# Row-wise attention norms from the fourth token block on, in a fused linear-attention and two-layer MLP kernel on one Trainium2 core

## The chip, the core and the metric

The kernel runs on one core of a Trainium2 chip. A core has a matrix engine (TensorE, PE in the profile, with PEld for its weight loads), a vector engine (VectorE, DVE), a scalar engine (ScalarE, ACT), GpSimd (POOL) and SyncE (SP). Here POOL and SP do almost nothing but issue DMAs. Every engine works through its own instructions in program order and waits on semaphores for the others. The metric is the time on the device in microseconds; lower is better.

## The reference

```python
def _attn_ref(q, k, v, g_norm):                       # q, k, v: (8 batches, 8 heads, 576, 64) fp32
    kv = np.einsum('bhsd,bhse->bhde', k, v)           # 64x64 for each batch and head
    out = np.einsum('bhsd,bhde->bhse', q, kv)
    rms = np.sqrt(np.mean(out * out, axis=-1, keepdims=True) + 1e-06)
    return out / rms * g_norm                         # norm over the 64 values of a head

# x = attention output as (4608 tokens, 512); w_in (512, 2048), w_out (2048, 512), alpha (2048)
def _moe_ref(x, w_in, w_out, alpha):
    h = x @ w_in
    g = np.maximum(h, 0.0) + alpha * np.minimum(h, 0.0)
    return g @ w_out
```

## The kernel before

All matrix work is in fp16 with fp32 sums. The 4608 tokens are cut into nine blocks of 512 (`w` = 0 to 8; a batch has 576 tokens, so blocks and batches do not line up). The main loop `for w in range(1, NW)` runs 16 units `u` in each block. A unit does, in this program order:

- `m1_group(w, g)` (L391, L398, L402): four 128x512 matmuls give one 128-wide slice of the hidden layer in a PSUM bank. ACT takes the negative part (`m_sb`), DVE adds `beta * m_sb` to the bank and writes `gt`. From block 2 on two banks alternate, so the matmuls of unit u+2 wait until DVE has written `gt` of unit u.
- `unit_sums` and seven `prod_mm` (L546): the second layer of block w-1, written as seven half-size products over sums of tiles of `gt` and of `w_out`. `s_sum` makes the sums on DVE. Results collect in banks X, Y and Z, and `y_read` takes them out: `p1` and `c11` on ACT, `u2`, `u3`, `c22`, `c21` and `c12` on DVE. `Y_READS` says at which units; outputs are stored by SP.
- `attention(w + 1, u)`: one step of the attention of the next block. For each of the four head pairs: `step_kv` (five 128x128 matmuls and a masked multiply on DVE, L335), `step_ot` (the attention output with features on partitions, 128x512, L349, and its square on ACT, L355), and `step_ssq` (a 128x512 matmul with the block mask `mask16` sums the squares over each head and spreads the sums over its 64 partitions, L365; ACT turns them into `rstd`, L367; DVE multiplies output, `g_norm` and `rstd` into `xt`, L375).

The steps lie at units 3j+1, 3j+3 and 3j+5 for pair j. Batch w+2 is loaded by `load_gated` on POOL's queue: the remainder rows of q, then k, q and v. From batch 3 on q is turned by five DMA transposes on SP's queue (`dma_t`, L317), issued together at unit 11 of block w. POOL's next `load_gated` begins with the remainder rows of q, whose buffer the last of those five transposes must have read. ACT regroups k by pairs (`REG_AT`).

Block 0 is written out by hand. At the end of its first layer, after the hidden slice 14, DVE regroups k of batch 1 and clears a part of a k buffer, then writes `gt` of slice 15, whose bank a run of block 0's second layer needs.

The order on every engine is the order of the program text (`manual_schedule`); no planner moves anything.

Of the kernel before, what the change touches and what calls it, by code (L numbers as in the profile page):

```python
# [9 lines left out]
FP32 = mybir.dt.float32  # L10
FP16 = mybir.dt.float16
AF = mybir.ActivationFunctionType
ALU = mybir.AluOpType
# [4 lines left out]
def kernel(  # L18
# [11 lines left out]
    nc = tc.nc  # L30
# [5 lines left out]
    P = 128  # L36
# [11 lines left out]
    NC = D_MODEL // P  # L48
    assert NC == NPAIR and 0 < REM < P and P0 <= P and H % 4 == 0
    B_NAT = 3  # L50
    inv_d = 1.0 / D

    const_p = ctx.enter_context(tc.tile_pool(name="constp", bufs=1))
# [67 lines left out]
    bufs = []  # L121
    for i in range(NBUF):
        t = {}
        for nm in ("k", "v", "q"):
            n = 1 if nm == "v" else T0 if i == 0 else NT
            t[nm] = qkv_p.tile([P, n, H, D], FP16, name=f"{nm}sb{i}")
            if i > 0 or nm == "v":
                nc.vector.memset(t[nm][REM:P, n - 1, :, :], 0.0)
        bufs.append(t)
# [26 lines left out]
            )  # L156

    def buf_of(b, nm):
        return bufs[1 if nm == "q" and b >= B_NAT else b % NBUF][nm]

    def load_rem(b, nm):
        nc.gpsimd.dma_start(  # L162
# [2 lines left out]
        )  # L165

    def regroup(b, nm, h0, h1, eng=None):
        dst = bufs[b % NBUF][nm][:, 0:TPP, h0:h1, :].rearrange("p t h d -> p h t d")
        src = stages[b, nm][:, h0:h1, :, :]
        if eng is nc.scalar:  # L170
            nc.scalar.copy(out=dst, in_=src)
        else:
            (eng or nc.vector).tensor_copy(out=dst, in_=src)

    def load_batch(b, names=("k", "v", "q")):
        for nm in names:
            load_rem(b, nm)
            load_main(b, nm)
# [30 lines left out]
    def load_w_in(i):  # L209
# [4 lines left out]
        )  # L214
        w_in_sb.append(t)

    def load_w_out(i):
        t = w_p.tile([P, GW, D_MODEL], FP16, name=f"w_out_sb{i}")
        nc.gpsimd.dma_start(
            out=t[:],  # L220
            in_=moe_w_out[i * GW * P : (i + 1) * GW * P, :].rearrange("(g p) m -> p g m", p=P),
        )
        w_out_sb.append(t)
# [25 lines left out]
    load_batch(1, ("v",))  # L249
    load_w_out(2)  # L250
    load_w_out(3)
    load_batch(2, ("q", "k", "v"))


    warm_ps = ps_q.tile([P, W], FP32, name="warm_ps", tag="q")
# [18 lines left out]
    def pair_cols(b, nm, j):  # L274
        def f(t):
            n = rows(b)
            if nm == "v" and b == 0:
                h = 2 * j % HH
                return stages[b, nm, 2 * j // HH][0:n, h : h + 2, t, :]
            if nm == "v" and t < TPP:  # L280
                return stages[b, nm][:, 2 * j : 2 * j + 2, t, :]
            if nm == "v":
                return bufs[b % NBUF][nm][0:n, 0, 2 * j : 2 * j + 2, :]
            return bufs[b % NBUF][nm][0:n, t, 2 * j : 2 * j + 2, :]
        return f

    def step_t(b, j, pool=(ps_s, "s")):
        qs = pair_cols(b, "q", j)
        qt_ps = pool[0].tile([P, n_runs(b) * rows(b)], FP16, name="qt_ps", tag=pool[1])
        c = 0  # L290
        for t in range(n_runs(b)):
            n = rows(b)
            nc.tensor.matmul(  # L293
                out=qt_ps[:, c : c + n],
                lhsT=qs(t),
                rhs=ident16[0:n, 0:n],
                is_transpose=True,
                start=(t == 0),
                stop=(t == n_runs(b) - 1),
            )  # L300
            c += n
        if j == 0:
            qt_all[b] = attn_p.tile([P, NPAIR, S], FP16, name="qt_all")
        qts[b, j] = qt_all[b][:, j, :]
        if b == 0 and j < 2:
            nc.vector.tensor_copy(out=qts[b, j], in_=qt_ps[:, 0:S])
        else:
            nc.scalar.copy(out=qts[b, j], in_=qt_ps[:, 0:S])

    qt_all = {}  # L310

    def dma_t(b):
        qt = attn_p.tile([P, NPAIR, S], FP16, name="qt_all")
        for t in range(NT):
            c0, c1 = t * P, min((t + 1) * P, S)
            src = stages[b, "q"][:, t] if t < TPP else buf_of(b, "q")[0:REM, TPP]
            nc.sync.dma_start_transpose(  # L317
                out=qt[:, :, c0:c1], in_=src.rearrange("p h d -> p (h d)"),
            )
        for j in range(NPAIR):  # L320
            qts[b, j] = qt[:, j, :]

    def step_kv(b, j, pool=(ps_s, "s")):
        ks, vs = pair_cols(b, "k", j), pair_cols(b, "v", j)
# [37 lines left out]
    def ssq_mm(w, j, pool=(ps_s, "s")):  # L362
        ot_ps, sq = ots.pop((w, j))
        ssq_ps = pool[0].tile([P, W], FP32, name="ssq_ps", tag=pool[1])
        nc.tensor.matmul(out=ssq_ps[:], lhsT=mask16[:], rhs=sq[:], start=True, stop=True)  # L365
        rstd = attn_p.tile([P, W], FP32, name="rstd")
        nc.scalar.activation(  # L367
            out=rstd[:], in_=ssq_ps[:], func=AF.Abs_reciprocal_sqrt, bias=eps_t[:], scale=inv_d,
        )
        ots[w, j] = (ot_ps, rstd)  # L370

    def norm(w, j):
        ot_ps, rstd = ots.pop((w, j))
        xts[w, j] = xt_p.tile([P, W], FP16, name="xt", tag=f"xt{j}")
        nc.vector.scalar_tensor_tensor(  # L375
            out=xts[w, j][:], in0=ot_ps[:], scalar=g2col[:], in1=rstd[:],
            op0=ALU.mult, op1=ALU.mult,
        )

    gts = {}  # L380
# [8 lines left out]
    def m1_mm(h_ps, w, g, cs):  # L389
        for c in cs:  # L390
            nc.tensor.matmul(  # L391
                out=h_ps[:], lhsT=w_in_blk(c, g), rhs=xts[w, c][:],
                start=(c == 0), stop=(c == NC - 1),
            )

# [193 lines left out]
    Y_LIST = [(n, i) for n in Y_ORDER for i in range(2 * NK)]  # L589
    PER = len(Y_LIST) // NF  # L590
    Y_READS = {2: ("p1",), 5: ("u2",), 7: ("c11",), 9: ("u3",), 11: ("c22",), 14: ("c21",)}
    G_ORDER = [0, 1, 8, 9, 2, 3, 10, 11, 4, 5, 12, 13, 6, 7, 14, 15]


# [64 lines left out]
    ssq_mm(0, 3, h_at(2))  # L659
    norm(0, 2)  # L660
    norm(0, 3)
    first = [ps_h.tile([P, W], FP32, name="h_ps", tag=f"h{g}") for g in range(3)]
    for c in range(3):
        for g in range(2):
# [6 lines left out]
    for g in range(3, NF):  # L671
        m1_group(0, g, {3: S_POOL, 4: O_POOL, 5: O_POOL, 6: Q_POOL}.get(g))
        if g == 14:
            regroup(1, "k", 0, H)
            nc.vector.memset(bufs[0]["k"][REM:P, TPP, :, :], 0.0)


    ys = {}
# [66 lines left out]
    }  # L745

    def unit_sums(w, u):
        for back, n, k in S_AT.get(u, ()):
            if 1 <= w + back < NW:
                s_sum(w + back, n, k)  # L750

# [9 lines left out]
            ATT_1.setdefault(at, []).append((what, j))  # L761
    ATT = {"t": step_t, "kv": step_kv, "ot": step_ot, "ssq": step_ssq}

    def attention(w, u):
        if w < NW:
            for what, j in (ATT_1 if w == 2 else ATT_AT).get(u, ()):
                if what == "t" and w >= B_NAT:
                    continue
                if w < B or what in ("ot", "ssq"):
                    if w == 2 and what in ("kv", "ssq"):  # L770
                        pool = Q_POOL if j % 2 == 0 else S_POOL
                        (step_kv if what == "kv" else step_ssq)(w, j, pool)
                    else:
                        ATT[what](w, j)

    REG_AT = {8 + 2 * j: (("k", j),) for j in range(NPAIR)}

    Y3_AT = [(8, 8), (8, 8), (8, 8), (8, 9), (9, 9), (9, 10), (10, 10), (10, 10), (10, 11), (11, 11), (11, 12), (12, 12), (12, 13), (13, 14), (14, 16), (16, 16)]
    REG_2 = {2 * j: (("k", j),) for j in range(NPAIR)}
# [1 line left out]
    for w in range(1, NW):  # L781
        if w + 2 < B:
            load_gated(w + 2)
        for u in range(NF):
            m1_group(w, G_ORDER[u])
            if w > 1:
                unit_sums(w, u)
            if w == 1 and u == 2:
                regroup(2, "k", 0, H)
            if w == 1 and u == 3:  # L790
                dma_t(3)
            if w == 2 and u == 0:
                h_tags[0] = ("h1", "h2")
                h_turn[0] = 1
            if w > 2 and u == 0:
                y_read(w - 2, "c12")
            if w == 1:
                for i in range(*Y3_AT[u]):
                    y_mm(ys[3], 0, 3, i)
                    if i == NF - 1:  # L800
                        y_out(ys[3], 0, 3)
            else:
                for i in range(u * PER, (u + 1) * PER):
                    prod_mm(w - 1, *Y_LIST[i])
                for what in Y_READS.get(u, ()):
                    y_read(w - 1, what)
            attention(w + 1, u)
            if w == 1:
                for k in {5: (0,), 7: (1,)}.get(u, ()):
                    s_sum(1, 1, k)  # L810
                    s_sum(1, 2, k)
            if w + 2 < B:
                for nm, j in REG_AT.get(u, ()) if w > 1 else ():
                    regroup_pair(w + 2, nm, j)
                if u == 11 and w > 1:
                    dma_t(w + 2)
            if w == 2:
                for nm, j in REG_2.get(u, ()):
                    regroup_pair(3, nm, j)
                if u < 2:  # L820
                    s_sum(1, u + 1, 2)
# [48 lines left out]
```

## Time and profile before

| what | value |
|---|---|
| median of 3 runs | 282.61 us (282.56 to 283.07) |
| profiled execution | 282.48 us, span 280.7 us |
| PE busy | 274.0 us (98%), 1888 matmuls |
| DVE busy | 219.9 us (78%) |
| ACT busy | 157.0 us (56%) |
| granted TensorE clock | 1.0 |

The time of an execution is 1.8 us above the span of its profile. Blocks 2 to 6 take 28.9 us each in the trace, block 7 27.8 us. Busy times are merged, and an instruction's duration is longer than its distance to the next one on the same engine, since instructions overlap in the pipeline: a 128x512 matmul is shown with 379 ns and follows its neighbour after 216 ns. Sums over time are therefore made with distances between starts, not with durations.

### The profile page before, as it was taken

How to read it: one execution, taken by the hardware profiler on the slowest of the kernel's cores; microseconds unless marked ns; L12 is line 12 of the kernel's file. 1: busy time of each engine (PE TensorE's matmuls, PEld its weight loads, DVE VectorE, ACT ScalarE, POOL GpSimd, SP SyncE). 2: the span in 40 equal slices, each digit the busy share in tenths (PEclk: the TensorE clock that was granted, in tenths of full speed). 3: DMA queues.
4: the chain of work that ended last, by engine and by line, in shares of the span. 5: the costliest groups of instructions: out<-in, count | busy, mean ns of one | idle time of the engine just before them, and what ended most of it. 6: DMA issues, size and time to landing. Idle time of an engine off the chain costs nothing.

```text
span 280.7 us, 4978 instructions
## 1 busy us (share of the span) xinstructions
PE 274.0 (98%) x1888; PEld 173.8 (62%) x1888; DVE 219.9 (78%) x418; ACT 157.0 (56%) x268; POOL 61.9 (22%) x85
## 2 busy tenths in 40 slices
PE   7899999999999999999999999999999999999995
PEld 3444444555666676666666666666666666666784
DVE  6668729898788877887889787978887888787872
ACT  3567437788676545764576456745564566443310
POOL 8843332740720046007300450000000000000000
PEclk9999999999999999999999999999999999999999
DMA  8999999999793469947953697330112011201223
GB/s 163 199 207 196 197 201 193 191 140 169 91 171 69 104 72 165 152 112 120 165 91 97 121 152 122 93 106 1 40 37 75 2 37 37 77 0 37 77 76 114
DMA packets 77628, 31.37 MB, mean 112 GB/s; under 512 B 45780, under 2 KB 77284, under 8 KB 77604
## 3 DMA queue, kind: packets, MB, share of 16 engines
q0 software_dynamic: 55600, 18.85, 58.8%
q1 hardware_dynamic: 21108, 11.25, 15.0%
q10 hardware_dynamic: 896, 0.95, 1.0%
q8 instruction: 15, 0.25, 0.4%
q14 instruction: 9, 0.07, 0.1%
HBM read 36.71 MB, written 9.44 MB: 164 GB/s over the span
## 4 chain that ended last, share of the span: by engine, by line
PE 92%; DMA 5%; DVE 1%; ACT 0%; issue 0%; DVEq 0%
PE h_ps L391 42%; PE yY L546 15%; PE yZ L546 10%; PE yX L546 10%; DMA vst<-in_v_dram 5%; PE kv_ps L327 3%; PE ot_ps L349 3%; PE ssq_ps L365 3%; PE y L416 2%; PE warm_ps L259 2%; PE qt_ps L293 1%; DVE xt L375 1%; ACT rstd L367 0%; DVE kv_sb L335 0%; DVE ksb L193 0%
## 5 line engine op out<-in xcount | busy, mean ns | idle before, releaser
L391 PE MATMUL h_ps<-xt,w_in_sb 128*128 128x512 f16 x576 | 145.2, 379 | 0.2
L402 DVE SCALAR_TENSOR_TENSOR gt<-m_sb,beta_sb,h_ps 128x512 f16<-128x512 f32 x144 | 106.9, 746 | 39.9 <-ACT m_sb L398 38.1
L398 ACT ACTIVATE m_sb<-h_ps 128x512 f32<-128x512 f32 x144 | 86.0, 598 | 74.8 <-PE h_ps L391 60.2
L391 PEld LDWEIGHTS <-w_in_sb 128*128 128x128 f16 x576 | 54.8, 98 | 46.4 <-issue 1.0
L546 PEld LDWEIGHTS <-s 128*128 128x128 f16 x512 | 50.1, 98 | 19.3
L546 PEld LDWEIGHTS <-gt 128*128 128x128 f16 x384 | 37.6, 98 | 14.8
L546 PE MATMUL yY<-wsum,s 128*128 128x256 f16 x256 | 36.3, 273 | 0.0
L546 PE MATMUL yX<-w_out_sb,gt 128*128 128x256 f16 x256 | 35.1, 273 | 0.0
L355 ACT ACTIVATE sq_sb<-ot_ps 128x512 f16<-128x512 f32 x36 | 21.2, 598 | 16.7 <-PE ot_ps L349 16.6
L367 ACT ACTIVATE rstd<-ssq_ps,eps_t 128x512 f32<-128x512 f32 x36 | 24.7, 690 | 9.7 <-PE ssq_ps L365 9.2
L375 DVE SCALAR_TENSOR_TENSOR xt<-ot_ps,g2col,rstd 128x512 f16<-128x512 f32 x36 | 26.6, 745 | 3.2 <-ACT rstd L367 3.2
L162 POOL DMA_DIRECT2D qsb<-in_q_dram x7 | 4.9, 699 | 78.3 <-DMA qt_all<-qsb 76.3
L153 POOL DMA_DIRECT2D qst<-in_q_dram x20 | 17.7, 922 | 1.9 <-DMA vst<-in_v_dram 1.9
L546 PE MATMUL yZ<-wsum,s 128*128 128x256 f16 x128 | 17.6, 273 | 0.0
L546 PE MATMUL yZ<-w_out_sb,s 128*128 128x256 f16 x128 | 17.6, 273 | 0.0
L546 PE MATMUL yY<-wsum,gt 128*128 128x256 f16 x128 | 17.6, 273 | 0.0
L416 PE MATMUL y<-w_out_sb,gt 128*128 128x512 f16 x64 | 16.8, 379 | 0.5 <-DMA w_out_sb<-in_moe_w_out_dram 0.5
L349 PE MATMUL ot_ps<-qt_all,kv_sb 128*128 128x512 f16 (+7 forms) x64 | 13.6, 286 | 0.4 <-DVE kv_sb L335 0.3
L498 DVE TENSOR_TENSOR s<-s,gt 128x512 f16<-128x512 f16 x32 | 13.5, 421 | 0.5
L327 PEld LDWEIGHTS <-ksb 128*128 128x128 f16 (+1 forms) x164 | 11.5, 98 | 3.7 <-DVE ksb L193 1.1
L365 PE MATMUL ssq_ps<-sq_sb,mask 128*128 128x512 f16 x36 | 13.6, 379 | 0.1
L496 DVE TENSOR_TENSOR s<-gt 128x512 f16<-128x512 f16 x32 | 13.3, 419 | 0.1
(66 smaller groups left out, 206.6 us busy)
## 6 DMA issues: line engine op xcount, KB each, us to landing
out_dram<-y_sb SPq DMA_DIRECT2D x19, 256.0 KB, 2.2
kst<-in_k_dram POOLq DMA_DIRECT2D x7, 512.0 KB, 7.8
vst<-in_v_dram POOLq DMA_DIRECT2D x7, 512.0 KB, 9.9
qst<-in_q_dram POOLq DMA_DIRECT2D x20, 128.0 KB, 7.2
w_out_sb<-in_moe_w_out_dram POOLq DMA_DIRECT2D x4, 512.0 KB, 16.1
out_dram<-y_sb SPq DMA_DIRECT2D x25, 64.0 KB, 4.2
w_in_sb<-in_moe_w_in_dram POOLq DMA_DIRECT2D x3, 512.0 KB, 11.6
out_dram<-y_sb SPq DMA_DIRECT2D x9, 128.0 KB, 2.1
```

What stands on the lines that cost most here:

```text
L153: nc.gpsimd.dma_start(out=st[:, t, :, :], in_=srcs["q"][b, :, t * P : (t + 1) * P, :].rearrange("h p d -> p h d"),)
L327: nc.tensor.matmul(out=kv_ps[:], lhsT=ks(t), rhs=vs(t), start=(t == 0), stop=(t == n_runs(b) - 1),)
L349: nc.tensor.matmul(out=ot_ps[:, n0 - w * W : n1 - w * W], lhsT=kvs[b, j][:], rhs=qts[b, j][:, n0 - b * S : n1 - b * S], start=True, stop=True,
L355: nc.scalar.activation(out=sq[:], in_=ot_ps[:], func=AF.Square)
L365: nc.tensor.matmul(out=ssq_ps[:], lhsT=mask16[:], rhs=sq[:], start=True, stop=True)
L367: nc.scalar.activation(out=rstd[:], in_=ssq_ps[:], func=AF.Abs_reciprocal_sqrt, bias=eps_t[:], scale=inv_d,)
L375: nc.vector.scalar_tensor_tensor(out=xts[w, j][:], in0=ot_ps[:], scalar=g2col[:], in1=rstd[:], op0=ALU.mult, op1=ALU.mult,)
L391: nc.tensor.matmul(out=h_ps[:], lhsT=w_in_blk(c, g), rhs=xts[w, c][:], start=(c == 0), stop=(c == NC - 1),)
L398: nc.scalar.activation(out=m_sb[:], in_=h_ps[:], func=AF.Relu, scale=-1.0)
L402: nc.vector.scalar_tensor_tensor(out=gts[w, i][:, r, :], in0=m_sb[:], scalar=beta_sb[:, g : g + 1], in1=h_ps[:], op0=ALU.mult, op1=ALU.add,)
L416: nc.tensor.matmul(out=y[:], lhsT=gt_cols(w, g, a * P, (a + 1) * P), rhs=w_out_blk(g), start=(g == 0), stop=(g == NF - 1),)
L546: nc.tensor.matmul(out=bank, lhsT=lhs, rhs=rhs, start=fresh, stop=(c == NK - 1), skip_group_check=True,)
```

## The change

From block 4 on (`W_ROW = 4`), whose attention runs inside blocks 3 to 7, the attention output is computed with tokens on partitions. `rows_mm` makes 128 tokens x 512 features with q as the stationary operand and kv as the moving one: four 128x128 matmuls, or eight where the 128 tokens span two batches. ACT squares it, DVE sums the squares of each head (`rows_ssq`), ACT makes 128x8 values of `rstd`, DVE multiplies with these broadcast along the head, and SP turns the result by a DMA transpose into `xt`. The mask matmul falls away there. `g_norm` no longer enters the norm from block 3 on; `scale_w_in` multiplies it into `w_in` in place, in block 2, after each unit's use.

The steps of these blocks lie at other units (`ATT_ROW`): kv at 0 and 1, the tiles at 2, 4, 6 and 8, their norms at 5, 7, 9 and 11; `dma_t` is spread over units 7, 9 and 11. `u3` and `c22` are read at the beginning of units 10 and 12 instead of the end of 9 and 11, and some sums move (`S_ROW`). q needs two row buffers instead of three, and the load of batch 2 stands later in the text; the two `qt_sb` are fixed, with 64 zero columns on either side, cleared in block 0. `dma_t(3)` moves to unit 12 of block 1 with its pieces in another order.

```diff
-        for nm in ("k", "v", "q"):
+        for nm in ("k", "v", "q") if i < 2 else ("k", "v"):
...
-        return bufs[1 if nm == "q" and b >= B_NAT else b % NBUF][nm]
+        return bufs[min(b, B_NAT) % 2 if nm == "q" else b % NBUF][nm]
...
+    def scale_w_in(g):
+        i = max(n for n, f0 in enumerate(IN_CUTS[:-1]) if f0 <= g * P)
+        f0 = g * P - IN_CUTS[i]
+        blk = w_in_sb[i][:, :, f0 : f0 + P]
+        nc.vector.tensor_scalar(
+            out=blk, in0=blk, scalar1=g2col[:], scalar2=None, op0=ALU.mult,
+        )
...
-    load_batch(2, ("q", "k", "v"))
...
+    PAD = P // 2
+    qt_sb = [const_p.tile([P, NPAIR, PAD + S + PAD], FP16, name=f"qt_sb{i}") for i in range(2)]
+
+    def dma_t(b, ts=tuple(range(NT))):
+        qt = qt_sb[b % 2][:, :, PAD : PAD + S]
+        for t in ts:
...
     def norm(w, j):
         ot_ps, rstd = ots.pop((w, j))
+        if w >= W_ROW - 1:
+            nc.vector.tensor_mul(out=xt_cols(w, j), in0=ot_ps[:], in1=rstd[:])
+            return
...
+    def rows_mm(w, i):
+        n0 = w * W + i * P
+        b, r = divmod(n0, S)
+        pool, tag = (ps_s, "s") if i == 2 else (ps_o, "o")
+        o_ps = pool.tile([P, W], FP32, name="or_ps", tag=tag)
+        for j in range(NPAIR):
+            cols = o_ps[:, j * P : (j + 1) * P]
+            if r + P <= S:
+                c = PAD + r
+                nc.tensor.matmul(
+                    out=cols, lhsT=qt_sb[b % 2][:, j, c : c + P], rhs=kvs[b, j][:],
+                    start=True, stop=True,
+                )
+            else:
+                assert r + PAD == S
+                nc.tensor.matmul(
+                    out=cols, lhsT=qt_sb[b % 2][:, j, S : S + P], rhs=kvs[b, j][:],
+                    start=True, stop=False,
+                )
+                nc.tensor.matmul(
+                    out=cols, lhsT=qt_sb[(b + 1) % 2][:, j, 0:P], rhs=kvs[b + 1, j][:],
+                    start=False, stop=True,
+                )
+        sq = attn_p.tile([P, W], FP16, name="sq_sb")
+        nc.scalar.activation(out=sq[:], in_=o_ps[:], func=AF.Square)
+        ots[w, "r", i] = (o_ps, sq)
+
+    def rows_ssq(w, i):
+        o_ps, sq = ots.pop((w, "r", i))
+        ssq = attn_p.tile([P, H], FP32, name="ssq_r")
+        nc.vector.tensor_reduce(
+            out=ssq[:], in_=sq[:].rearrange("p (h d) -> p h d", h=H),
+            axis=mybir.AxisListType.X, op=ALU.add,
+        )
+        ots[w, "r", i] = (o_ps, ssq)
+
+    def rows_rs(w, i):
+        o_ps, ssq = ots.pop((w, "r", i))
+        rstd = attn_p.tile([P, H], FP32, name="rstd_r")
+        nc.scalar.activation(
+            out=rstd[:], in_=ssq[:], func=AF.Abs_reciprocal_sqrt, bias=eps_t[:], scale=inv_d,
+        )
+        ots[w, "r", i] = (o_ps, rstd)
+
+    def rows_norm(w, i):
+        o_ps, rstd = ots.pop((w, "r", i))
+        xr = attn_p.tile([P, H, D], FP16, name="x_rows", tag="rstd" if i % 2 else "x_rows")
+        nc.vector.tensor_tensor(
+            out=xr[:], in0=o_ps[:].rearrange("p (h d) -> p h d", h=H),
+            in1=rstd[:].unsqueeze(2).to_broadcast([P, H, D]), op=ALU.mult,
+        )
+        xt_cols(w, 0)
+        nc.sync.dma_start_transpose(
+            out=xts[w][:, :, i * P : (i + 1) * P], in_=xr[:].rearrange("p h d -> p (h d)"),
+        )
...
+    R_ROW = {2: ("p1",), 5: ("u2",), 7: ("c11",), 14: ("c21",)}
+    R_FIRST = {10: "u3", 12: "c22"}
...
+    load_batch(2, ("q", "k", "v"))
     first = [ps_h.tile([P, W], FP32, name="h_ps", tag=f"h{g}") for g in range(3)]
...
-            nc.vector.memset(bufs[0]["k"][REM:P, TPP, :, :], 0.0)
+            for nm in ("k", "q"):
+                nc.vector.memset(bufs[0][nm][REM:P, TPP, :, :], 0.0)
+            for t in qt_sb:
+                nc.vector.memset(t[:, :, 0:PAD], 0.0)
+                nc.vector.memset(t[:, :, PAD + S : PAD + S + PAD], 0.0)
...
+    for at, what in (
+        (4, ((-1, 3, 3),)), (6, ((0, 1, 0),)), (7, ((-1, 4, 0),)), (8, ((0, 2, 0),)),
+        (9, ((-1, 4, 1),)), (10, ()), (11, ((-1, 4, 2),)), (12, ((-1, 4, 3),)),
+        (13, ((0, 1, 1), (0, 2, 1))), (15, ((0, 1, 2), (0, 2, 2))),
+    ):
+        S_ROW[at] = what
...
+    def row_kv(w, j):
+        step_kv(w, j, O_POOL if j % 2 else S_POOL)
...
+        ("kv", (0, 0, 1, 1)), ("mm", (2, 4, 6, 8)), ("ssq", (4, 6, 8, 10)),
+        ("rs", (5, 7, 9, 11)), ("norm", (5, 7, 9, 11)),
...
+    QT_AT = {7: (0, 1), 9: (2, 3), 11: (4,)}
...
+        if W_ROW <= w < NW:
+            for what, j in ATT_ROW.get(u, ()):
+                if what != "kv" or w < B:
+                    ROWS[what](w, j)
+            if w + 1 < B:
+                dma_t(w + 1, QT_AT.get(u, ()))
...
-    REG_AT = {8 + 2 * j: (("k", j),) for j in range(NPAIR)}
+    REG_AT = {9 + 2 * j: (("k", j),) for j in range(NPAIR)}
...
+            if w >= W_ROW - 1 and u in R_FIRST:
+                y_read(w - 1, R_FIRST[u])
             m1_group(w, G_ORDER[u])
+            if w == W_ROW - 2:
+                scale_w_in(G_ORDER[u])
...
-            if w == 1 and u == 3:
-                dma_t(3)
...
+            if w == 1 and u == 12:
+                dma_t(3, (3, 4, 0, 1, 2))
...
-                if u == 11 and w > 1:
+                if u == 12 and 1 < w < W_ROW - 1:
                     dma_t(w + 2)
```

More of the change, by code (lines that the diff above doesn't have):

```diff
@@ L50 @@
     B_NAT = 3
+    W_ROW = 4
     inv_d = 1.0 / D
@@ L167, in regroup @@
     def regroup(b, nm, h0, h1, eng=None):
-        dst = bufs[b % NBUF][nm][:, 0:TPP, h0:h1, :].rearrange("p t h d -> p h t d")
+        dst = buf_of(b, nm)[:, 0:TPP, h0:h1, :].rearrange("p t h d -> p h t d")
         src = stages[b, nm][:, h0:h1, :, :]
@@ L282, in f @@
             if nm == "v":
-                return bufs[b % NBUF][nm][0:n, 0, 2 * j : 2 * j + 2, :]
-            return bufs[b % NBUF][nm][0:n, t, 2 * j : 2 * j + 2, :]
+                return buf_of(b, nm)[0:n, 0, 2 * j : 2 * j + 2, :]
+            return buf_of(b, nm)[0:n, t, 2 * j : 2 * j + 2, :]
         return f
@@ L301, in step_t @@
             c += n
-        if j == 0:
-            qt_all[b] = attn_p.tile([P, NPAIR, S], FP16, name="qt_all")
-        qts[b, j] = qt_all[b][:, j, :]
+        qts[b, j] = qt_sb[b % 2][:, j, PAD : PAD + S]
         if b == 0 and j < 2:
@@ L308, in step_t @@
             nc.scalar.copy(out=qts[b, j], in_=qt_ps[:, 0:S])
[L310 to L314, printed above, removed]
+    PAD = P // 2
[3 more added lines that the diff above has]
+        for t in ts:
             c0, c1 = t * P, min((t + 1) * P, S)
@@ L320, in dma_t @@
         for j in range(NPAIR):
-            qts[b, j] = qt[:, j, :]
+            qts[b, j] = qt_sb[b % 2][:, j, PAD : PAD + S]
     def step_kv(b, j, pool=(ps_s, "s")):
@@ L365, in ssq_mm @@
         nc.tensor.matmul(out=ssq_ps[:], lhsT=mask16[:], rhs=sq[:], start=True, stop=True)
-        rstd = attn_p.tile([P, W], FP32, name="rstd")
+        rstd = attn_p.tile([P, W], FP32, name="rstd", tag="rstd")
         nc.scalar.activation(
@@ L373, in norm, with xt_cols @@
         ot_ps, rstd = ots.pop((w, j))
-        xts[w, j] = xt_p.tile([P, W], FP16, name="xt", tag=f"xt{j}")
+        if w >= W_ROW - 1:
+            nc.vector.tensor_mul(out=xt_cols(w, j), in0=ot_ps[:], in1=rstd[:])
+            return
         nc.vector.scalar_tensor_tensor(
-            out=xts[w, j][:], in0=ot_ps[:], scalar=g2col[:], in1=rstd[:],
+            out=xt_cols(w, j), in0=ot_ps[:], scalar=g2col[:], in1=rstd[:],
             op0=ALU.mult, op1=ALU.mult,
+        )
+    def xt_cols(w, j):
+        if w not in xts:
+            xts[w] = xt_p.tile([P, NPAIR, W], FP16, name="xt")
+        return xts[w][:, j, :]
@@ L391, in m1_mm @@
             nc.tensor.matmul(
-                out=h_ps[:], lhsT=w_in_blk(c, g), rhs=xts[w, c][:],
+                out=h_ps[:], lhsT=w_in_blk(c, g), rhs=xts[w][:, c, :],
                 start=(c == 0), stop=(c == NC - 1),
@@ L745 @@
     }
+    S_ROW = dict(S_AT)
+    for at, what in (
[3 rows of a table added]
+    ):
+        S_ROW[at] = what
     def unit_sums(w, u):
-        for back, n, k in S_AT.get(u, ()):
+        for back, n, k in (S_ROW if W_ROW - 1 <= w < NW - 1 else S_AT).get(u, ()):
             if 1 <= w + back < NW:
@@ L762 @@
     ATT = {"t": step_t, "kv": step_kv, "ot": step_ot, "ssq": step_ssq}
-    def attention(w, u):
-        if w < NW:
+    def row_kv(w, j):
+        step_kv(w, j, O_POOL if j % 2 else S_POOL)
+    ATT_ROW = {}
+    for what, ats in (
+        ("kv", (0, 0, 1, 1)), ("mm", (2, 4, 6, 8)), ("ssq", (4, 6, 8, 10)),
+        ("rs", (5, 7, 9, 11)), ("norm", (5, 7, 9, 11)),
+    ):
+        for j, at in enumerate(ats):
+            ATT_ROW.setdefault(at, []).append((what, j))
+    ROWS = {"kv": row_kv, "mm": rows_mm, "ssq": rows_ssq, "rs": rows_rs, "norm": rows_norm}
+    QT_AT = {7: (0, 1), 9: (2, 3), 11: (4,)}
+    def attention(w, u):
+        if W_ROW <= w < NW:
[4 more added lines that the diff above has]
+                dma_t(w + 1, QT_AT.get(u, ()))
+        elif w < NW:
             for what, j in (ATT_1 if w == 2 else ATT_AT).get(u, ()):
@@ L804 @@
                     prod_mm(w - 1, *Y_LIST[i])
-                for what in Y_READS.get(u, ()):
+                for what in (R_ROW if w >= W_ROW - 1 else Y_READS).get(u, ()):
                     y_read(w - 1, what)
             attention(w + 1, u)
+            if w == 1 and u == 12:
+                dma_t(3, (3, 4, 0, 1, 2))
             if w == 1:
```

## The prediction

> **What bounds the kernel now.** I read first the page's busy row, then PE's list of waits, then the table by stage (cut at the starts of blocks 3 to 7), then PE's instructions in order of time inside block 4.
>
> ```profile
> span 280.7 us, 4978 instructions
> PE 274.0 (98%) x1888; PEld 173.8 (62%) x1888; DVE 219.9 (78%) x418; ACT 157.0 (56%) x268; POOL 61.9 (22%) x85
> ...
> PE y L416 <- DMA w_out_sb<-in_moe_w_out_dram: 0.5, 1, 0.5
> PE kv_ps L327 <- DMA vst<-in_v_dram: 0.4, 1, 0.4
> ...
> 95.72:124.61 28.89, 28.89 (x210) 19.50 (x208) 23.65 (x46) 17.38 (x31) 7.33 (x9) 1.00 0.99 126
> 124.61:153.51 28.90, 28.90 (x211) 19.46 (x208) 23.66 (x46) 17.39 (x31) 7.32 (x9) 1.00 0.88 115
> ...
> 131.40 0.38 PE L349 MATMUL ot_ps<-qt_all,kv_sb 128*128 128x320 f16 x2
> 131.62 1.03 PE L391 MATMUL h_ps<-xt,w_in_sb 128*128 128x512 f16 x4
> ...
> 133.25 0.39 PE L327 MATMUL kv_ps<-vst,ksb 128*128 128x128 f16 x4
> 133.47 0.22 PE L327 MATMUL kv_ps<-vsb,ksb 128*128 128x128 f16 x1
> 133.53 1.03 PE L391 MATMUL h_ps<-xt,w_in_sb 128*128 128x512 f16 x4
> 134.39 0.93 PE L546 MATMUL yX<-w_out_sb,gt 128*128 128x256 f16 x7
> 135.16 0.38 PE L365 MATMUL ssq_ps<-sq_sb,mask 128*128 128x512 f16 x1
> 135.37 0.59 PE L391 MATMUL h_ps<-xt,w_in_sb 128*128 128x512 f16 x2
> ```
>
> The stage rows (length, then PE, PEld, DVE, ACT, POOL busy, clock) show PE busy for the whole of 28.89 us, and no wait of PE lies after block 1. So PE's own instructions are the time: one taken out of blocks 3 to 7 is worth its distance to the next, until another engine makes PE wait. By start distances: 0.865 us for four `h_ps` matmuls, 0.765 for seven products, 0.28 for the five of a kv step (56 ns each), 0.22 for an `ot` step, 0.21 for an `ssq` step (0.216 by four in 0.865). 16 x 1.63 + 4 x (0.28 + 0.22 + 0.216) = 28.9: the block, without gaps.
>
> DVE comes next: 23.66 of 28.90 us.
>
> ```profile
> L402 DVE SCALAR_TENSOR_TENSOR gt<-m_sb,beta_sb,h_ps 128x512 f16<-128x512 f32 x16 | 11.9, 747 | 5.2 <-ACT m_sb L398 5.1
> L375 DVE SCALAR_TENSOR_TENSOR xt<-ot_ps,g2col,rstd 128x512 f16<-128x512 f32 x5 | 3.7, 744 | 0.0
> L568 DVE TENSOR_TENSOR u<-yY,p 128x512 f32<-128x512 f32 x2 | 1.4, 684 | 0.0
> ```
>
> **PE, part by part.** Removed: 4 mask matmuls in each of five blocks, 20 x 0.216 = 4.32 us. Replaced: the 20 `ot` steps of 0.22 by 20 tiles of four 128x128 matmuls. None has q as weights yet, but the kv row has the same form, with new weights for each matmul: 4 x 0.056 = 0.224, so +0.1 in all. Added: tokens 2816 to 2943 and 3968 to 4095 cross a batch border (576 x 5 = 2880, 576 x 7 = 4032), four more matmuls each, +0.45. Net 3.75 us less, 0.77 of a block that then takes about 28.07.
>
> Here a rule speaks against the change. The Trainium skill (TensorE: Matmul & The Clock Gate, "Back-to-back issue gap") gives about 81 ns per matmul in a stream of weight load and 128-column matmul. By it the 88 row matmuls take 7.1 us instead of 4.9, and the net is 1.5 us. The kv row, in this place at clock 1.00, has 56; I take that.
>
> **DVE, blocks 3 to 7.** New: four reductions a block, 512 fp16 values to 8. No row shows one. Nearest below: the fp16 sums (about 0.34 between starts, two values a cycle or more); above: the PSUM `xt` at 0.66. The skill's perf-mode tier table (VectorE: DVE Perf Modes) says that `tensor_reduce` has only the one-element-a-cycle form, so fp16 gains nothing: nearest is then the fp32 add `u` (0.61 to the next). I take 0.60; at the rate of the fp16 sums it would be 0.34. The norm becomes a two-operand multiply, 0.60 for 0.66. Per block +4 x 0.60 - 4 x 0.06 = +2.2: about 25.9 busy of 28.07. It fits as an average; what counts is the queue. DVE may begin `gt` 1.70 us after its matmuls begin (126.31 for 124.61), and its result comes 0.75 later, while the bank is wanted by the unit after next, about 3.3 us after. Slack is about 0.8 us. Units 9 to 14 with distances 0.66 (`gt`), 0.34 (sum), 0.61 (`u3`, `c22`), 0.60 (norm, reduction), in us from the block's start:
>
> | unit | matmuls start | gt may start | DVE does | free at |
> |---|---|---|---|---|
> | 9 | 16.67 | 18.37 | gt, sum, norm | 19.97 |
> | 10 | 18.30 | 20.00 | u3 first, gt, reduction | 21.84 |
> | 11 | 19.93 | 21.63 | gt, sum, norm | 23.44 |
> | 12 | 21.56 | 23.26 | c22 first, gt from 24.05 | 24.71 |
> | 14 | 24.81 | | needs gt of 12, there at 24.80 | |
>
> DVE is idle 0.25 us ahead of unit 9 and again from unit 15, so a block's backlog does not reach the next. The worst place has 0.01 us of slack. I charge 0.1 us a block, 0.5 in all. At unit 1 the third kv step wants the bank of the first, whose multiply ends at about 3.6 by the same count, against PE's 3.82: free. All sums, `u2` and `c21` are there over 0.5 us before use.
>
> ACT loses 4 x 0.69 and gains four small instructions (128x8; between nothing and a 128x512's 0.69, taken as 0.25): it has room. The later k regroups (units 9 to 15) still end before kv at the next block's start.
>
> **SP and POOL.** SP gets four more transposes a block.
>
> ```profile
> 92.83 5.14 SPq L317 DMA_TRANSPOSE qt_all<-qst  x4
> 98.07 2.60 SPq L317 DMA_TRANSPOSE qt_all<-qsb  x1
> ...
> 102.30 0.70 POOL L162 DMA_DIRECT2D qsb<-in_q_dram  x1 [23.18 <-DMA qt_all<-qsb]
> 102.99 0.70 POOL L162 DMA_DIRECT2D ksb<-in_k_dram  x1
> 103.66 0.91 POOL L144 DMA_DIRECT2D kst<-in_k_dram  x1
> 104.53 3.54 POOL L153 DMA_DIRECT2D qst<-in_q_dram  x4
> ```
>
> Each holds SP 1.2 to 1.3 us and lands 2.3 after its issue (2.3 to 5.0 beside loads). In block 4 SP has from 15.5: three `c11` stores of 0.57 (to 17.2), x tile 1 (18.4), two q pieces (20.8), x tile 2 (22.0), two q pieces (24.4), x tile 3 (25.6), landing at 26.7. The next block starts at 28.07: 1.35 us to spare. The q pieces wait for loads of that batch. In block 3 these begin when the last q piece of batch 4 has landed, 102.30 as now, so q is issued from 104.5 and lands 7.9 later, 112.4 to 115.1. SP reaches those pieces at about 114.2 and 117.8, so they do not hold it; its last x tile lands at about 122.7 against 123.8. I charge 0.2 us for this handover. Later the remainder of q is turned earlier than now, and loads with it. Behind the x tile stand the last q piece and stores of `c22` and `c21`; four output buffers, one block of time, nobody waits.
>
> **Block 2.** 16 scalings, 512 fp16 values each. Nearest row: the DVE copy of 2048 fp16 values, 0.69 us, thus four values a cycle with about 0.15 fixed; scaled down about 0.2 between starts. Other end: one value a cycle, 0.60. At 0.2 DVE goes from 24.1 to 27.3 of 28.9, with a backlog of 0.4 us at most by the count above: nothing. At 0.60 it would be bound and cost 3.5 us; for the range.
>
> **Blocks 0 and 1.** Five memsets of 0.2 to 0.27 (row: 128x128 in 0.165, next start after 0.23), 1.1 us, stand ahead of the last `gt` of block 0 (31.25 to 32.00), and PE wants its bank at 32.03. So PE will wait about 1.1 us there. But it now waits 0.5 for `w_out` until 34.99 and 0.4 for v until 38.12, plus 0.25 for q regrouped at 33.1; these loads stay in place on POOL, and take the delay up: cost 0, up to 1.1 if that cover were gone. `dma_t(3)` waits now, at unit 3, until the last `ot` step of block 1 at 62.94 has read the old q; at unit 12 it waits for the same step. Its last piece is issued at 68.6, wanted at 73.6. Free.
>
> **Sum.** Against the profiled execution, 282.48 us (span 280.7 and 1.8 around it, 0.13 under the median): -3.75 + 0.5 + 0.2 = -3.05, so 279.4; on the median 282.61, **279.6 us**.
>
> **Rivals.**
> - DVE is slower than counted. If the reduction takes 0.9 (a start-up for each of eight heads, say), the same table gives `gt` of unit 12 at 25.40 and a wait of 0.6 us in each block, 3.0 in all: 282.0. For it: 0.01 us of slack. Against: the plain one-a-cycle rate. With the scaling at two values a cycle the loss is in the same class. Between, 281.
> - The weight loads are not hidden (81 ns): 281.8. Against: the kv row.
> - Slower: SP is held by its transposes. Seven stand from x tile 1 to x tile 3; the trace has issues of 1.94 and 2.60 beside loads. At 1.7 each the last x tile lands 3.5 us later, at 30.2, and blocks 4 to 7 each begin 2.1 us late: 282.6 - 3.05 + 8.5 = 288. It decides from 1.55 us an issue (wait 0.94 x 4 = 3.75). Against: 1.2 in blocks 3, 4 and 6.
> - That the mask matmuls do not go: excluded by the text, `step_ssq` isn't called for w of 4 and more.
>
> **The numbers.** Forecast 0.60 (279 to 280.6); DVE or weight loads take part of it 0.24 (280.6 to 282.0); nothing left 0.05; SP 0.11. What a measurement of this kernel can tell from no change is about 0.2%, 0.57 us. Faster 0.84, same 0.05, slower 0.11. The low end, 278.5, is the net of 3.75 with no stall and some noise; the high end, 281.7, reaches into the DVE case.
>
> **What would show it.** In the stage rows, blocks 3 to 7 at about 28.1 to 28.3 with PE full; no L365 rows there; `or_ps` at 56 ns; the reduction near 0.69 long. Waits of `h_ps` on DVE `gt` above 2 us in all would be the first rival; of `h_ps` on a DMA of `xt` the third. Block 2 above 29.2 us would put the scaling wrong; block 0 longer, the cover. A time over 282 would mean that one of these is the bound.

## The result, and the profile after

The changed kernel takes 281.12 us (median of 4 runs, 280.86 to 281.85) against 282.8 for the kernel before: a ratio of 0.9944, 95% interval 0.9922 to 0.9967. That is faster, by 1.7 us; 3.0 were forecast. The saving on PE came as forecast; two losses elsewhere took back nearly half of it.

The profiled execution took 280.86 us, with a span of 279.0. First its busy row and, from the table by stage, blocks 2 to 7 (length, then PE, PEld, DVE, ACT and POOL busy with instruction counts, clock, DMA share, GB/s).

```profile
PE 270.3 (97%) x1920; PEld 173.4 (62%) x1920; DVE 233.6 (84%) x458; ACT 148.4 (53%) x268; POOL 62.0 (22%) x85
...
66.84:96.12 29.28, 29.06 (x210) 19.27 (x208) 27.55 (x62) 19.46 (x35) 7.32 (x9) 1.00 0.94 112
96.12:125.50 29.38, 28.21 (x214) 19.16 (x212) 26.72 (x52) 16.26 (x32) 7.33 (x9) 1.00 1.16 140
125.50:153.77 28.27, 28.27 (x216) 19.45 (x217) 24.36 (x47) 15.19 (x30) 7.32 (x9) 1.00 1.05 140
153.77:181.82 28.05, 28.05 (x214) 19.24 (x212) 25.54 (x49) 15.73 (x32) 7.33 (x9) 1.00 1.05 143
181.82:210.10 28.28, 28.28 (x219) 19.45 (x217) 25.54 (x49) 14.21 (x28) 0.00 (x0) 1.00 0.23 66
210.10:237.03 26.93, 26.93 (x194) 18.12 (x192) 24.68 (x45) 13.76 (x27) 0.00 (x0) 1.00 0.21 60
```

Blocks 4 to 7 are what the sum asked for: 28.05, or 28.28 with a tile that spans two batches, and 26.93 for block 7 (27.8 before). PE is busy for the whole of each. (The wanted length of block 3 is 28.05 too.) Blocks 2 and 3 are longer than before, 29.28 and 29.38 us against 28.89. That is where 1.72 of the 3.75 us went. PE's list of waits from block 2 on names both places:

```profile
PE h_ps L461 <- DVE s L566: 1.2, 1, 1.2
PE yY L616 <- DVE s L568: 0.2, 1, 0.2
```

The first is at the start of block 4, and its releaser is misnamed: it was an x tile. PE in order of time there, then SP from the first x tile of block 3 on:

```profile
122.54 1.03 PE L461 MATMUL h_ps<-xt,w_in_sb 128*128 128x512 f16 x4
123.41 0.93 PE L616 MATMUL yZ<-w_out_sb,s 128*128 128x256 f16 x7
125.50 1.02 PE L461 MATMUL h_ps<-xt,w_in_sb 128*128 128x512 f16 x4 [1.17 <-DVE s L566]
```

```profile
109.53 1.24 SPq L446 DMA_TRANSPOSE xt<-x_rows  x1
111.46 1.80 SPq L497 DMA_DIRECT2D out_dram<-y_sb  x3
113.36 1.25 SPq L446 DMA_TRANSPOSE xt<-x_rows  x1
114.71 2.74 SPq L324 DMA_TRANSPOSE qt_sb<-qst  x2
117.54 2.52 SPq L446 DMA_TRANSPOSE xt<-x_rows  x1
120.16 2.61 SPq L324 DMA_TRANSPOSE qt_sb<-qst  x2
122.86 1.22 SPq L446 DMA_TRANSPOSE xt<-x_rows  x1
124.17 1.20 SPq L324 DMA_TRANSPOSE qt_sb<-qsb  x1
```

DVE has the last x tile of block 3 ready at about 119.6. SP is still issuing q pieces and reaches it at 122.86. The trace has no landing for this one; at the usual 2.4 us it would be there at about 125.3. PE, which was done with block 3 at 124.2, begins block 4 at 125.50. The first three x tiles landed 5.6 to 8.3 us after their issue, beside the loads of batch 5; the median over all 20 is 2.4.

The second wait is in block 2: a product of unit 2 waits for the sum that DVE begins at 71.80, behind a scaling (`w_in_sb`), another sum and a kv multiply.

```profile
70.82 0.53 DVE L222 TENSOR_SCALAR w_in_sb<-w_in_sb,g2col 128x512 f16<-128x512 f16 x1
71.27 0.41 DVE L568 TENSOR_TENSOR s<-s,gt 128x512 f16<-128x512 f16 x1
71.60 0.28 DVE L342 TENSOR_TENSOR kv_sb<-kv_ps,mask 128x128 f16<-128x128 f32 x1
71.80 0.41 DVE L568 TENSOR_TENSOR s<-s,gt 128x512 f16<-128x512 f16 x1
...
72.27 0.28 PE L616 MATMUL yY<-wsum,s 128*128 128x256 f16 x1 [0.22 <-DVE s L568]
```

DVE, in block 5 (start 153.77), agrees with the table of the prediction. First its groups there with their mean durations, then the place that was counted as the tightest:

```profile
L441 DVE TENSOR_TENSOR x_rows<-or_ps,rstd_r 128x512 f16<-128x512 f32 x4 | 2.7, 682 | 0.0
L424 DVE TENSOR_REDUCE ssq_r<-sq_sb 128x8 f32<-128x512 f16 x4 | 2.7, 678 | 0.0
...
177.17 0.68 DVE L650 TENSOR_TENSOR y_sb<-yZ,u 128x512 f32<-128x512 f32 x1
177.76 0.73 DVE L472 SCALAR_TENSOR_TENSOR gt<-m_sb,beta_sb,h_ps 128x512 f16<-128x512 f32 x1
...
178.57 1.03 PE L461 MATMUL h_ps<-xt,w_in_sb 128*128 128x512 f16 x4
```

`gt` of unit 12 begins 24.0 us into the block and ends at 178.49; the matmuls of unit 14, which need its bank, begin at 178.57, on time.

### The profile page after: what moved, and what is told of

Same layout as the page of the kernel before. It is cut to its first block, busy times and chain, and to the rows that moved or that the text cites. A ratio compares the mean times of both kernels' runs of the same rounds, so it can differ in the third digit from the quotient of the medians.

```text
span 279.0 us, 5157 instructions
## 1 busy us (share of the span) xinstructions
PE 270.3 (97%) x1920; PEld 173.4 (62%) x1920; DVE 233.6 (84%) x458; ACT 148.4 (53%) x268; POOL 62.0 (22%) x85
## 4 chain that ended last, share of the span: by engine, by line
PE 87%; DMA 7%; DVE 3%; ACT 1%; issue 1%; DVEq 0%; POOLq 0%
PE h_ps L461 42%; PE yY L616 15%; PE yZ L616 10%; PE yX L616 9%; DMA vst<-in_v_dram 7%; PE kv_ps L334 3%; PE y L486 2%; PE or_ps L403 1%; PE ot_ps L356 1%; PE ssq_ps L372 1%; DVE gt L472 1%; PE qt_ps L301 1%; DVE xt L384 1%; ACT rstd L374 0%; ACT m_sb L468 0%
## 5 line engine op out<-in xcount | busy, mean ns | idle before, releaser
L418 ACT ACTIVATE sq_sb<-or_ps 128x512 f16<-128x512 f32 x20 | 11.9, 597 | 5.7 <-PE or_ps L403 4.6
L362 ACT ACTIVATE sq_sb<-ot_ps 128x512 f16<-128x512 f32 x16 | 9.3, 599 | 9.3 <-PE ot_ps L356 9.3
L441 DVE TENSOR_TENSOR x_rows<-or_ps,rstd_r 128x512 f16<-128x512 f32 x20 | 13.6, 682 | 0.0
L424 DVE TENSOR_REDUCE ssq_r<-sq_sb 128x8 f32<-128x512 f16 x20 | 13.6, 678 | 0.0
L342 DVE TENSOR_TENSOR kv_sb<-kv_ps,mask 128x128 f16<-128x128 f32 x32 | 8.4, 284 | 5.9 <-PE kv_ps L334 5.9
L572 DVE TENSOR_TENSOR s<-gt,s 128x512 f16<-128x512 f16 x32 | 13.2, 417 | 0.0
```

What stands on the lines that cost most here:

```text
L418: nc.scalar.activation(out=sq[:], in_=o_ps[:], func=AF.Square)
L424: nc.vector.tensor_reduce(out=ssq[:], in_=sq[:].rearrange("p (h d) -> p h d", h=H), axis=mybir.AxisListType.X, op=ALU.add,)
L441: nc.vector.tensor_tensor(out=xr[:], in0=o_ps[:].rearrange("p (h d) -> p h d", h=H), in1=rstd[:].unsqueeze(2).to_broadcast([P, H, D]), op= ...
L572: nc.vector.tensor_sub(out=t[:], in0=a12, in1=sums[w, 2, k][:])
```

## The experiments

The theory after reading the traces: PE saves its 3.75 us, and loses 1.2 to 1.3 at the handover from block 3 to 4, where the last x tile stands behind q pieces on SP's queue, and 0.4 in block 2, where a sum stands behind scalings on DVE. The main rival for the handover: not SP's order but the loads of batch 5, beside which every transpose is slow.

**again**: the changed kernel once more.

> The changed kernel once more, beside the three variants. Theory: of the 3.75 us that PE saves, about 1.2 go where block 4 waits for its last x tile and 0.4 in block 2, so 281.1 again, with block 3 at 29.4 us and block 2 at 29.3. Rival: these waits are chance of one execution; then blocks 2 and 3 come out at other lengths here and the time moves by up to 1 us.

281.14 us, ratio 0.9948 (0.9933 to 0.9962). The handover wait is no accident of one execution, but its size varies: block 3 takes 30.89 us in this profile, which is of an execution of 282.61 us, with a wait of 2.7 us, and this time the releaser is named. Block 2 takes 29.11 us here and not 29.28, so part of its loss varies too.

```profile
PE h_ps L461 <- DMA xt<-x_rows: 2.7, 1, 2.7
```

SP held the third x tile for 2.71 us and the next two q pieces for 3.96. The 22 runs lie between 280.03 and 283.56 (the longest at a granted clock of 0.992, the next at 282.61); those of the kernel before between 281.92 and 283.45.

**q_behind**: the q pieces behind the last x tile, in blocks 3 to 5 (block 6 has none).

```diff
-    QT_AT = {7: (0, 1), 9: (2, 3), 11: (4,)}
+    QT_AT = {11: (0, 1, 2, 3, 4)}
```

> All five q transposes of blocks 3 to 6 go at unit 11, behind the last x tile on SP. Theory (SP's queue: four q pieces, 5.4 us, stand ahead of the last x tile): that tile is issued at about 119.5 in place of 122.9, lands before block 4 begins, block 3 falls from 29.4 to 28.2 us, the time to 279.9. Rival (the DMA engines are busy with the loads of batch 5, and a transpose lands 7 to 8 us after its issue wherever it stands): the last x tile still lands at 125 or later, block 3 stays at 29.4, 281.1. A third possibility: q lands later, so the loads of the next batch start later and the wait turns up in block 4 or 5.

279.51 us (279.1 to 279.56), ratio 0.9881 (0.9866 to 0.9896). SP in order of time:

```profile
113.41 7.45 SPq L446 DMA_TRANSPOSE xt<-x_rows  x3
120.95 5.14 SPq L324 DMA_TRANSPOSE qt_sb<-qst  x4
```

The last x tile is issued at 119.7. No PE wait is left from block 2 on, and block 3 takes 28.05 us. The x tiles still landed 2.5 to 8.8 us after issue: traffic was the same, changing the order was enough to take the wait away. The third possibility, a wait in a later block, did not come. These four runs lie within 0.5 us and the five of both within 0.9, where 22 of the changed kernel spread over 3.5. That fits a handover that makes the time vary, but it is few runs.

**rem_first**: the loads of batch 5 begin earlier, SP's order in block 3 unchanged.

```diff
-                    dma_t(w + 2)
+                    dma_t(w + 2, (3, 4, 0, 1, 2))
```

> In block 2 the remainder piece of q goes second among the five transposes, not last, so the load of batch 5 may begin some 4 us earlier (98 to 99 in place of 102.6). SP's order in block 3 is untouched. Theory of SP's queue alone: the q pieces still stand ahead of the last x tile, each at 1.3 us in place of up to 2.5, so the last x tile is issued about 1.3 to 2 us earlier and most of the 1.2 us wait goes: 280.0 to 280.4. Rival (load traffic makes the transposes slow): all of the wait goes, and x tiles in block 3 land 2.3 to 5 us after issue in place of 7.9: 279.9. If the load does not matter: 281.1.

279.94 us, ratio 0.9902 (0.9886 to 0.9918). The load of batch 5 begins at 97.75 in place of 102.56, the last x tile is issued at 121.93, 0.9 earlier than in the changed kernel (1.3 to 2 were forecast), and block 3 takes 28.34 us: 0.3 of the wait stays. x tiles of block 3 still landed up to 8.5 us after issue, so neither sign of the rival came. The time lies between the two forecasts and does not decide. Of the transposes that stood ahead of the last x tile one was slow, a q piece of 1.89 us at 116.03, when all but the last of the loads (v, at 117.02) had landed.

**q_only_5**: k and v of batch 5 not loaded, order kept.

```diff
+        if b == 5:
+            load_q(b)
+            for nm in ("k", "v"):
+                stages[b, nm] = stages[b - 1, nm]
+            return
         load_rem(b, "k")
```

> The changed kernel, but of batch 5 only q is loaded; its k and v are left out (those of batch 4 stand in, as far as they are in memory), so the result is not the reference's for the tokens of batch 5. SP's order is as in the changed kernel. Theory of traffic (SP's transposes are held up and land late because the loads of batch 5 run beside them in block 3): x tiles in block 3 land 2.3 to 4 us after issue, not 7 to 8, each piece holds SP 1.2 to 1.3 us, and the wait at block 4 goes: block 3 at 28.1 us, 279.9. Rival (SP is slow by the number of its transposes alone): SP still held 2.5 us and more by single pieces, the last x tile issued at about 122.9 and block 3 at 29 us or above: 281.1.

280.38 us, ratio 0.9919 (0.9901 to 0.9937). SP in block 3:

```profile
113.75 2.15 SPq L451 DMA_TRANSPOSE xt<-x_rows  x1
116.00 2.52 SPq L329 DMA_TRANSPOSE qt_sb<-qst  x2
118.61 1.22 SPq L451 DMA_TRANSPOSE xt<-x_rows  x1
119.94 2.52 SPq L329 DMA_TRANSPOSE qt_sb<-qst  x2
122.55 1.22 SPq L451 DMA_TRANSPOSE xt<-x_rows  x1
```

Without these loads x tiles land 2.4 us after issue (one after 3.3), and the third x tile and the q pieces hold SP 1.2 us each. Block 3 takes 28.62 us: 0.76 of the 1.33 us went with the loads, 0.57 stayed. Neither side had all of it. But what stayed is not the mere number of SP's instructions. The second x tile held SP for 2.15 us with no load in flight. At 1.2 us, the last x tile would have been issued at about 121.6 and landed at about 124.0 (an estimate from 122.55, 2.15 and 2.4), before PE was done with block 3 at 124.6. In block 5 of the changed kernel the same order costs no wait: there each of these transposes holds SP 1.2 us. So the wait takes both, the order and a slow transpose; changing the order is enough to remove it (q_behind).

The loads are not all that goes with a slow transpose. In the changed kernel a q piece at 97.43 held SP for 2.20 us, 5 us before the loads of batch 5 begin. The second and third line are the DMA queues from 97.8 to 98.5; the queue of POOL's loads (q0) has nothing there:

```profile
97.43 2.20 SPq L324 DMA_TRANSPOSE qt_sb<-qst  x1
...
q8 instruction: 1, 0.02, 11.0%
q1 hardware_dynamic: 72, 0.01, 8.7%
```

The queue that the profile calls `q8 instruction` has 15 packets of 16 KB in an execution. In the ten traces together, 300 transposes held SP while no load was in flight. The 262 of them with no such packet in flight either held it 1.19 to 1.25 us; of the 38 with one, 30 held it over 1.5, up to 2.60. The 2.15 here is one of these. Beside loads, 12 of 130 held SP over 1.5 us, and 10 of the 12 met such a packet as well, the 2.52 of the changed kernel and the 1.89 of rem_first among them. No run takes these packets away, so that they are a cause is not shown. That loads alone stretch the queue is not what the traces say.

**scale_last**: in block 2 the scaling stands behind the sums and kv multiplies of its unit.

```diff
-            if w == W_ROW - 2:
-                scale_w_in(G_ORDER[u])
...
                     s_sum(1, u + 1, 2)
+            if w == W_ROW - 2:
+                scale_w_in(G_ORDER[u])
```

> Block 2 scales its w_in slice at the end of each unit, behind the sums and kv multiplies, not ahead of them. Theory: the 0.4 us of block 2 is a product of unit 2 that waits for a sum which stands behind two scalings on DVE, so block 2 falls from 29.3 to 28.9 us and the time by 0.4, to 280.7. Rival (the scaling as such overloads DVE in block 2, wherever it stands): block 2 stays at 29.3.

Block 2 takes 28.89 us (66.40 to 95.29), as before the change, so its loss was the place of the scaling and not DVE's load. The time, 281.2, ratio 0.9943 (0.9926 to 0.996), shows none of it, where 280.7 was forecast. In the trace block 4 waits for its x tile:

```profile
PE h_ps L461 <- DMA xt<-x_rows: 2.5, 1, 2.5
```

An earlier end of block 2 may thus only lengthen that wait. But the interval is some 0.5 us wide on either side, and the wait differs from one execution to the next, so a gain of 0.2 to 0.4 cannot be excluded.

**both**: q_behind and scale_last together.

> The q pieces behind the x tiles (as in q_behind) and the scaling behind the sums (as in scale_last). Theory: the two losses are one behind the other; with the handover free, block 2 at 28.89 us now counts too. Blocks 2 to 7 at 28.89, 28.05, 28.27, 28.05, 28.27, 26.93, which is the 3.75 us of PE to a few hundredths: 279.2 to 279.3, some 0.2 to 0.3 under q_behind. Rival (an earlier end of block 2 only makes block 4 wait for its x tile again, as it did in scale_last): 279.5, with a wait for xt at the start of block 4.

279.49 us (278.77 to 279.7), ratio 0.9887 (0.9868 to 0.9906). The stages:

```profile
67.08:95.98 28.90, 28.90 (x209) 19.41 (x208) 27.24 (x61) 19.48 (x35) 7.37 (x9) 1.00 0.96 118
95.98:124.03 28.05, 28.05 (x214) 19.23 (x212) 25.50 (x50) 15.73 (x32) 7.33 (x9) 1.00 1.13 134
```

Blocks 2 to 7 take 168.48 us against 172.23 before: 3.75 less, to the hundredth, with no PE wait. The time is the rival's 279.5, 0.2 above the forecast, but the wait for xt that the rival needs is not there. The 0.2 us that block 2 gains over q_behind (28.90 for 29.11) are in the trace; in the medians, 279.49 and 279.51, they cannot be seen.

**both_reduce2**: the reductions made twice.

```diff
+        ssq2 = attn_p.tile([P, H], FP32, name="ssq_2")
+        nc.vector.tensor_reduce(
+            out=ssq2[:], in_=sq[:].rearrange("p (h d) -> p h d", h=H),
+            axis=mybir.AxisListType.X, op=ALU.add,
+        )
         ots[w, "r", i] = (o_ps, ssq)
```

> As both, with each of the 20 reductions made twice; the second result goes nowhere. Theory of the prediction's table (DVE's slack up to unit 14 is about 0.1 us in each of blocks 3 to 7): three of the four doubled reductions lie ahead of unit 12, 1.8 us less the idle 0.25 ahead of unit 9, so gt of unit 12 comes 1.5 us late and each of the five blocks gets 1.3 to 1.5 us longer: 285.7 to 286.8. Rival (by the busy sum DVE has over 2 us of idle time in a block, which takes it up): 279.3, or at most 1 us more.

287.85 us, ratio 1.0184 (1.0168 to 1.0201): 8.4 over both, 1.5 to 1.75 in each of the five blocks (29.80 in place of 28.05). Block 4:

```profile
126.13:155.94 29.81, 29.20 (x219) 19.42 (x216) 27.59 (x53) 15.74 (x32) 7.32 (x9) 1.00 0.98 129
```

DVE is idle for 2.2 us of this block and still sets its length. In block 5 nearly all of that idle time lies in units 0 to 4, ahead of the first reduction, and `gt` of unit 12 begins 25.75 us into the block in place of 24.0. The table by units foretold the size (1.3 to 1.5) a little low: the forecast took three of the four reductions to lie ahead of unit 12, and in the trace all four do. The sum of busy times foretold next to nothing.

**q_behind_t3**: q_behind, with `dma_t(3)` in the old order of its pieces.

```diff
-                dma_t(3, (3, 4, 0, 1, 2))
+                dma_t(3)
```

> As q_behind, with the five pieces of dma_t(3) in the old order (remainder last), still at unit 12 of block 1. POOL then begins to issue the loads of batch 4 about 1.2 us later (71.8 in place of 70.4). Theory (the scalings of block 2's first units are long, 0.53 and 0.83 us in place of 0.35, where POOL issues DMAs at the same moment): the scaling of unit 1 at about 71 is 0.35 long again, the sum of unit 1 comes about 0.2 earlier, and block 2 falls from 29.11 to 28.9 us; a later scaling grows in its stead, where it has slack. Rival (their length has nothing to do with POOL): 0.5 again in unit 1 and block 2 at 29.1. The time stays within 0.3 us of 279.5 in both cases; the trace decides.

281.36 us (280.92 to 283.36), ratio 0.9979 (0.995 to 1.0008): 1.8 us over q_behind, where at most 0.3 were expected. SP in block 1, then PE in block 2:

```profile
56.97 7.73 SPq L324 DMA_TRANSPOSE qt_sb<-qst  x4
64.80 1.24 SPq L324 DMA_TRANSPOSE qt_sb<-qsb  x1
```

```profile
71.58 0.38 PE L334 MATMUL kv_ps<-vst,ksb 128*128 128x128 f16 x4 [1.02 <-DMA vst<-in_v_dram]
```

With fixed buffers each piece waits only for the readers of its own columns. Block 2 begins in the last 128 columns of batch 1, so pieces 0 to 2 have nobody to wait for. They are issued at 56.97, 58.59 and 60.05, beside the loads of batch 3, at 1.3 to 1.4 us each; the fourth of the line above, piece 3, only at 63.51, after the last `ot` step. They land 5.2 to 8.9 us after issue, and v of that batch lands 12.4 us after its issue (9.7 in q_behind), too late for the first kv step of block 2. In the changed kernel piece 3 comes first, waits for the last `ot` step of block 1 (63.25) and keeps the others behind it until the loads are nearly done. The order that looked free is a brake, and is worth 1.8 us by the medians (block 2 of the trace is 30.34 us long in place of 29.11). The question that the run was made for it could not settle: block 2 was disturbed by the wait for v, and in q_behind, from which it starts, the scaling of unit 1 was 0.35 us long already.

## Why the prediction was right or wrong

- **PE, -3.75 us.** Right, and shown in full by both. (A block became 0.84 us shorter, or 0.62 with a tile that spans two batches; the 0.77 of the text is neither, nor the mean of 0.75.) The row matmuls follow each other every 56 ns, as the kv row said (four `or_ps` from 159.77 to 160.00), not 81 as the Trainium skill (TensorE: Matmul & The Clock Gate, "Back-to-back issue gap") has it. That rival is out.
- **DVE, blocks 3 to 7, +0.5.** Too cautious: 0. The reduction was 0.678 us long, the norm 0.682, against 0.42 for an fp16 sum of the same length, so the one-element-a-cycle rule was the right end. The count of 24.05 us for `gt` of unit 12 came out at 24.0, and both_reduce2 showed that the slack is thin. (The rival with a reduction of 0.9 us, at 0.6 a block, lets only two of the four reductions delay unit 12.)
- **The step that failed: "I charge 0.2 us for this handover".** It measured 1.33 us in the profiled execution (29.38 less 28.05) and 2.84 in that of again (30.89 less 28.05). The walk along SP's queue named the right instructions, and reached the first two q pieces at 114.2 against 114.71. Then it gave every transpose 1.2 us, where the trace of before already had holds of 1.94 and 2.60 and landings of 5.0. SP took 8.15 us for the five transposes from there to the last x tile, where the walk had 6.0; the third x tile alone took 2.52. The slow transposes had been put into a rival (all blocks, 288 us) in place of the one block where they met the handover. It was that rival's mechanism, in block 3 alone. The prediction read the 1.94 and 2.60 as "beside loads"; the trace of before has no load in flight at either, and an instruction packet at both. Its "1.2 in blocks 3, 4 and 6" does not hold either, since the 1.94 is in block 4; and only blocks 3 to 5 of the changed kernel have q pieces, so the rival's four late blocks are one too many. That the order is the remedy is shown (q_behind, both); why single transposes are slow stays open.
- **Block 2, "nothing".** The second miss, 0.39 us; the prediction's own sign of it, block 2 above 29.2 us, came true. The rate was nearly right: 0.35 us long, some 0.26 between starts for the 0.2 counted. The count looked at banks and at the averages, and not at the one sum that a product needs in the next unit: `s` for the pair k=2 of block 1, made in unit 1 behind two scalings and a kv multiply and needed in unit 2. The second of the two was 0.53 us long in place of 0.35, but that is the smaller part: where both were 0.35 (again, q_behind, rem_first), block 2 still took 29.11 us, 0.22 more than before.
- **Blocks 0 and 1, 0.** Right. PE waited 0.46 us for the last `gt` of block 0 at 33.13 (some 1.1 were foretold), and kv began at 38.12 in both kernels: the cover held. `dma_t(3)` waited for the same step, as said, but only in its new order.
- **The sum.** 3.75 less 1.33 less 0.39 is 2.03, which is what blocks 2 to 7 gained (172.23 to 170.19). The span fell by 1.76 only, since its end came 0.27 us later after PE's last product than before; the cause of that stays open. The 0.5 us kept for DVE and not needed hid a part of the two misses, which is luck.

## What to carry to other kernels

Walk the queue that stands between a producer and the start of the next stage as carefully as the engine that is bound, with the long durations that single instructions of it show in the trace and not only the usual one, and put what the next stage needs ahead of what the stage after that needs. What is saved ahead of a handover that makes the next stage wait may not show in the time until the handover is free (scale_last alone showed no gain). Where an engine is nearly full, count it unit by unit up to the tightest consumer: at a busy share of 91%, 2.4 us more of DVE work made a block 1.5 to 1.75 us longer.

## What the hardware showed that was not expected

A DMA transpose of 128x512 fp16 values holds SP 1.2 us and mostly lands 2.3 to 2.4 us after its issue when no load is in flight. Beside the loads of a batch it landed after up to 9.6 us (again), yet most still held SP 1.2 to 1.4. Holds over 1.5 us nearly all (40 of 42 in the ten traces) met a packet of the instruction queue; why is open. The loads suffer as well: v of batch 3 landed 12.4 us after its issue beside early transposes, and 9.7 without (one trace each).

An in-place scaling of 512 fp16 values took 0.35 us, and 0.38 to 0.83 in some cases, all while POOL was issuing DMAs (nine traces). The Trainium skill (SBUF — State Buffer, "Who interferes with whom") says that a DVE instruction in a two-port mode, which `tensor_scalar` can enter, and GpSimd block each other at a shared pair of ports. The traces fit that, but others ran at 0.35 while POOL was issuing, and no run here isolates it.
